# Longer rows for two weight loads, another way to turn the head outputs into columns, and a reordered middle, in a one-token decode block

## The chip, the cores and the metric

The kernel runs on one core of a Trainium2 chip. The metric is the device time of one execution in microseconds (us). Each kernel was executed several times. Every execution has its own span (first to last instruction, about 1.8 us shorter than the time) and its own mean granted clock of TensorE.

The executions of these kernels do not lie around one value: they fall into groups one to three microseconds apart. The label "fast" or "slow" that an execution carries is given by a rule (over 1.5% above the fastest execution of the same kernel is slow).

## The reference, cut to what matters

One token `x` of 576 values is normalised; its result feeds an attention over the last 4,096 positions of a cache (32 query heads on 16 key/value heads of 128) and a gated MLP. The results are added.

```python
xn = layernorm(x)                                   # 1 x 576
q  = xn @ wq                                        # 576 x 4096
p  = softmax(q . K[last 4096] / sqrt(128))          # 16 kv heads, 2 queries each
o  = p . V[last 4096]                               # 32 heads x 128
z  = gelu(xn @ w_in)                                # 576 x 4608, halves z1 and z2
h  = z1 * (w_sp * layernorm(z2) + b_sp)
out = x + o @ wo + h @ w_out                        # 4096 x 576, 2304 x 576
```

All data are bfloat16. Nearly all of the 51 MB that are read are read once: K and V are 33.6 MB, the four weight matrices 17.4 MB.

## The kernel before: the parts that matter

All large loads are issued from the SP queue, in one order that is the order of use: wq, w_in, then K and V in four groups ("quads") of four kv heads, then w_out and wo. K and V tiles of 32 KB a partition share three buffers, so a load can be issued only after the last reader of the tile that lay in its buffer.

```python
KV_BUFS = 3
...
nc.sync.dma_start(wq_t[:], wrows(A_wq, 0, 4))
nc.sync.dma_start(wq_h[:], whalf(A_wq))
for t in range(2):
    nc.sync.dma_start(win_t[t][:], wrows(B_w_in, 2 * t, 2 * t + 2))   # 18 KB a partition each
nc.sync.dma_start(win_h[:], whalf(B_w_in))
load_k(0); load_k(1); load_v(0)
...
quad(0, lambda: gz.extend(z_columns()), lambda: z_gate(*gz))
load_k(2)                       # into the buffer of K0
quad(1, lambda: transpose_p(0), nothing)
load_v(1)                       # into the buffer of K1: waits for the end of quad 1
pv_quad(0)
transpose_p(1)
load_k(3)                       # into the buffer of V0
quad(2, lambda: o_rows(0), nothing)
load_v(2)
...
```

`quad(g)` transposes the K of quad g on TensorE and multiplies it with q; `z_columns` are 18 small fp32 matmuls that turn z into columns, with the GELU behind them. They stand in the middle of quad 0.

The tail, behind the last V:

```python
den = ...                       # sum of the softmax denominators: waits for a DVE reduce
o_rows(2)
pv_quad(3)
...
for n, (g, r0, r1) in enumerate(WO_CHUNKS):          # four pieces of 8 rows
    for r in range(r0, r1):
        project(oT_all[:, r, g:g + 1], wo_sb[n][:, r - r0, :])   # one row step: two matmuls, 256 and 320 columns
    spin(2 if n > 0 else 0)                          # dummy matmuls
```

`spin(n)` issues n dummy matmuls of 512 columns, which write an unused accumulator. They are there to keep TensorE's clock up.

The softmax here doesn't subtract the row's maximum and nothing guards it: scores larger than these inputs give would overflow.

Of the kernel before, what the change touches and what calls it, by code (L numbers as in the profile page):

```python
# [8 lines left out]
FP32 = mybir.dt.float32  # L9
BF16 = mybir.dt.bfloat16  # L10
ALU = mybir.AluOpType
ACT = mybir.ActivationFunctionType
AXX = mybir.AxisListType.X
# [3 lines left out]
D = 576  # L17
HQ = 32
# [4 lines left out]
F = 4608  # L23
# [10 lines left out]
NZ = 36  # L34
NZ1 = 18
KV_BUFS = 3
WO_CHUNKS = ((0, 0, 8), (1, 0, 8), (2, 0, 8), (3, 0, 8))
WOUT_CHUNKS = ((0, 0, 9), (1, 0, 5), (1, 5, 8), (1, 8, 9))


# [1 line left out]
def kernel(  # L42
# [14 lines left out]
    nc = tc.nc  # L57
    P = nc.NUM_PARTITIONS
# [13 lines left out]

    xrow = const.tile([1, D], BF16, name="xrow")
    sb_row = const.tile([1, 2], BF16, name="sb_row")
    nc.gpsimd.dma_start(xrow[:], x_flat)
    nc.gpsimd.dma_start(sb_row[:, 0:1], B_w_sp.flatten_outer_dims()[0:1, 0:1])
    nc.gpsimd.dma_start(sb_row[:, 1:2], B_b_sp.flatten_outer_dims()[0:1, 0:1])

    def wrows(src, t0, t1):
        return src[0:512, :].rearrange("(p t) c -> p t c", t=4)[:, t0:t1, :]  # L80
# [4 lines left out]
    wq_t = wpool.tile([P, 4, 4096], BF16, name="wq")  # L85
    wq_sb = [wq_t[:, t, :] for t in range(4)]
    wq_h = wpool.tile([P, 2048], BF16, name="wqh")
    win_t = [wpool.tile([P, 2, F], BF16, name=f"win{t}") for t in range(2)]
    win_sb = [win_t[t // 2][:, t % 2, :] for t in range(4)]
    win_h = wpool.tile([P, FH], BF16, name="winh")  # L90
    kn_tiles: dict = {}
    v_tiles: dict = {}
# [20 lines left out]

    nc.sync.dma_start(wq_t[:], wrows(A_wq, 0, 4))
    nc.sync.dma_start(wq_h[:], whalf(A_wq))
    for t in range(2):
        nc.sync.dma_start(win_t[t][:], wrows(B_w_in, 2 * t, 2 * t + 2))  # L117
    nc.sync.dma_start(win_h[:], whalf(B_w_in))
    load_k(0)
    load_k(1)  # L120
# [47 lines left out]
    def mean_rstd(stat_t, n, nm):  # L168
# [26 lines left out]
    nc.vector.reduce_sum(ind4[:], ident[:].rearrange("p (k h) -> p h k", h=4), axis=AXX)  # L195
    nc.vector.tensor_scalar_mul(
        own[:].rearrange("p (h e) -> p h e", e=2), ind4[:].unsqueeze(2).to_broadcast([P, 4, 2]), BIG)
    hmask = const.tile([P, 8], FP32, name="hmask")
    nc.vector.reduce_sum(hmask[:], ident[:].rearrange("p (h d) -> p h d", d=16), axis=AXX)
    psum_all = const.tile([P, HQ], FP32, name="psum_all")  # L200
    id4f = const.tile([P, 4], FP32, name="id4f")
    nc.vector.tensor_copy(id4f[:], ident[:, 0:P:32])
# [49 lines left out]
    def z_columns():  # L252
        zv = zrow[:].rearrange("p (c t) -> p t c", t=9)
        for t in range(9):
            nc.tensor.matmul(  # L255
                fin[:, MZ + 4 * t:MZ + 4 * t + 4], lhsT=zv[:, t, :], rhs=id4f[:], start=True, stop=True,
            )
        zsb = const.tile([P, NZ], FP32, name="zsb")
        nc.vector.tensor_copy(
            zsb[:].rearrange("p (i t) -> p i t", i=4),  # L260
            fin[:, MZ:MZ + NZ].rearrange("p (t i) -> p i t", i=4),
        )
        u = const.tile([P, NZ], FP32, name="u_gelu")
        nc.vector.tensor_mul(u[:], zsb[:], zsb[:])
        nc.vector.tensor_scalar(out=u[:], in0=u[:], scalar1=0.044715, scalar2=1.0, op0=ALU.mult, op1=ALU.add)
        nc.vector.tensor_mul(u[:], u[:], zsb[:])
        th = const.tile([P, NZ], FP32, name="th_gelu")
        nc.scalar.activation(th[:], u[:], ACT.Exp, scale=-2.0 * GELU_C)
        nc.vector.tensor_scalar_add(th[:], th[:], 1.0)
        nc.vector.reciprocal(th[:], th[:])  # L270
        G = const.tile([P, NZ], FP32, name="G_gelu")
        nc.vector.tensor_mul(G[:], th[:], zsb[:])
        statz = const.tile([P, 2], FP32, name="statz")
        nc.vector.reduce_sum(statz[:, 0:1], G[:, NZ1:NZ], axis=AXX)
        junk2 = work.tile([P, NZ1], FP32, name="junk")
        nc.vector.tensor_tensor_reduce(
            out=junk2[:], in0=G[:, NZ1:NZ], in1=G[:, NZ1:NZ], scale=1.0, scalar=0.0,
            op0=ALU.mult, op1=ALU.add, accum_out=statz[:, 1:2],
        )
        return G, statz  # L280
# [3 lines left out]
    def z_gate(G, statz):  # L284
        mvz = mean_rstd(statz, FH, "z")
        z2n = const.tile([P, NZ1], FP32, name="z2n")
        nc.vector.tensor_scalar(out=z2n[:], in0=G[:, NZ1:NZ], scalar1=mvz[:, 0:1], scalar2=mvz[:, 3:4],
                                op0=ALU.subtract, op1=ALU.mult)
        gv = const.tile([P, NZ1], FP32, name="gv")
        nc.vector.tensor_scalar(out=gv[:], in0=z2n[:], scalar1=sb_col[:, 0:1], scalar2=sb_col[:, 1:2],  # L290
                                op0=ALU.mult, op1=ALU.add)
        nc.vector.tensor_mul(hv[:], G[:, 0:NZ1], gv[:])

    w2pool = tc.alloc_tile_pool(name="w2pool", bufs=1, reuse_waits="tile")
    wo_sb = [w2pool.tile([P, r1 - r0, D], BF16, name=f"wo{g}_{r0}") for g, r0, r1 in WO_CHUNKS]
    wout_sb = [w2pool.tile([P, t1 - t0, D], BF16, name=f"wout{i}_{t0}") for i, t0, t1 in WOUT_CHUNKS]

    ptq = const.tile([P, 4, 2, 4, 32], BF16, name="ptq")
# [38 lines left out]
    def transpose_p(g):  # L337
        p_sb = p_tiles.pop(g)
        ptps = ps_t.tile([P, 8, P], BF16, name=f"ptps{g}", tag="tps")
        for b in range(2):  # L340
            for s in range(4):
                nc.tensor.transpose(ptps[:, 4 * b + s, :], p_sb[:, b, 128 * s:128 * (s + 1)], ident[:])
        for c in range(4):
            for b in range(2):
                nc.vector.tensor_tensor(  # L345
                    ptq[:, c, b, :, :].rearrange("p i (s x) -> p i s x", x=8),
                    ptps[:, 4 * b:4 * b + 4, :].rearrange("p s (i r) -> p i s r", i=4)[:, :, :, 8 * c:8 * c + 8],
                    own[:].unsqueeze(1).unsqueeze(1).to_broadcast([P, 4, 4, 8]),
                    ALU.min,
                )  # L350
        nc.vector.tensor_reduce(  # L351
            out=psum_all[:, 8 * g:8 * g + 8],
            in_=ptq[:].rearrange("p c b i (s x) -> p x (c b i s)", x=8),
            op=ALU.add, axis=AXX,
        )
# [24 lines left out]
    def quad(g, first, then):  # L380
        transpose_k(4 * g)
        first()
        for u in range(4 * g + 1, 4 * g + 4):
            transpose_k(u)
            if u == 4 * g + 1:
                then()
            scores(u - 1)
        scores(4 * g + 3)

    def pv_quad(g):  # L390
        for u in range(4 * g, 4 * g + 4):
            pv(u)
# [2 lines left out]
        pass  # L395

    gz: list = []
    quad(0, lambda: gz.extend(z_columns()), lambda: z_gate(*gz))
    load_k(2)
    quad(1, lambda: transpose_p(0), nothing)  # L400
    load_v(1)
    pv_quad(0)
    transpose_p(1)
# [11 lines left out]
            B_w_out[ZC * i:ZC * (i + 1), :].rearrange("(p t) n -> p t n", t=9)[:, t0:t1, :])  # L415

    load_wout(0)
    for n, (g, r0, r1) in enumerate(WO_CHUNKS):
        nc.sync.dma_start(
            wo_sb[n][:], A_wo[1024 * g:1024 * (g + 1), :].rearrange("(p r) n -> p r n", r=8)[:, r0:r1, :])  # L420
    for n in range(1, len(WOUT_CHUNKS)):
        load_wout(n)

    quad(3, lambda: o_rows(1), nothing)
    pv_quad(2)
    transpose_p(3)
    den = ps_t.tile([P, 512], FP32, name="den", tag="tps")
    nc.tensor.matmul(den[0:HQ, 0:1], lhsT=psum_all[:], rhs=ones_f[:, 0:1], start=True, stop=True)
    rden = const.tile([HQ, 1], FP32, name="rden")
    nc.vector.reciprocal(rden[:], den[0:HQ, 0:1])  # L430
    o_rows(2)
    pv_quad(3)
    def project(lhsT, rhs, first=False, last=False):
        for g, (c0, c1) in enumerate(halves):
            nc.tensor.matmul(  # L435
# [15 lines left out]
            project(hv[:, k:k + 1], wout_sb[n][:, t - t0, :], last=(k == NZ1 - 1))  # L451

    project(one_row[:, 0:1], xrow[:], first=True)
    o_rows(3)
    project_b(0, range(0, 5))
    spin(2)

    onb = const.tile([HQ, DH], BF16, name="onb")
    nc.vector.tensor_scalar_mul(onb[:], oall, rden[:])
    orep = w2pool.tile([HQ, 8, 8, 16], BF16, name="orep")  # L460
    orep_src = onb[:].rearrange("p (d r) -> p r d", r=8).unsqueeze(2).to_broadcast([HQ, 8, 8, 16])
    nc.vector.tensor_copy(orep[:, 0:4, :, :], orep_src[:, 0:4, :, :])
    nc.scalar.copy(orep[:, 4:8, :, :], orep_src[:, 4:8, :, :])
    oh = ps_t.tile([P, 8, 32], FP32, name="oh", tag="tps")
    for r in range(8):
        nc.tensor.matmul(
            oh[:, r, :], lhsT=orep[:, r, :, :].rearrange("p h d -> p (h d)"), rhs=ident[0:HQ, 0:HQ],
            start=True, stop=True)
    project_b(0, range(5, 9))
    spin(2)  # L470
    om = w2pool.tile([P, 32, 8], FP32, name="om")
    nc.vector.tensor_mul(
        om[:], oh[:].rearrange("p r (g h) -> p (r g) h", h=8), hmask[:].unsqueeze(1).to_broadcast([P, 32, 8]))
    oT_all = const.tile([P, 8, 4], BF16, name="oT_all")
    with nc.allow_low_precision("one of the eight addends is not zero"):
        nc.vector.reduce_sum(oT_all[:].rearrange("p r g -> p (r g)"), om[:], axis=AXX)

    for n, (g, r0, r1) in enumerate(WO_CHUNKS):
        for r in range(r0, r1):
            project(oT_all[:, r, g:g + 1], wo_sb[n][:, r - r0, :])  # L480
        spin(2 if n > 0 else 0)
    for n in range(1, len(WOUT_CHUNKS)):
        project_b(n, range(WOUT_CHUNKS[n][1], WOUT_CHUNKS[n][2]))
        spin(1 if n == 1 else 0)
# [36 lines left out]
```

## Time and profile before

| | before |
|---|---|
| median of the first 6 executions | 129.09 us (127.38 to 130.18) |
| those 6, sorted | 127.38, 127.68, 128.46, 129.72, 130.09, 130.18 |
| profiled execution | 127.53 us, span 125.7, in the lower group |
| first bulk packet starts, last ends | 1.74 us, 122.47 us |

From the profile's page, before: the span, then in 40 slices the granted clock of TensorE and the busy share of the DMA engines (tenths), the DMA queue's packets, MB and share of 16 engines, and the chain of work that ended last.

```profile
span 125.7 us, 2492 instructions
PEclk9999999975559599999999999995589997699999
DMA  5998999899999899999999989899899999999970
q1 hardware_dynamic: 3314, 50.96, 95.3%
DMA 57%; PE 25%; DVE 8%; ACT 5%; SPq 2%; issue 1%; ACTq 0%
```

The DMA engines are busy all the time. 50.96 MB in the 120.7 us of the stream are 422 GB/s. With each packet's bytes spread evenly over its duration, more than half of the single microseconds have 430 to 434 GB/s and none has more. The Trainium skill, "DMA: Bandwidth & Descriptors", section "Where 436 GB/s comes from", gives 435 GB/s as the ceiling of the ports into the on-chip memory, and this trace agrees with it. (The same section says that for loads from HBM a limit near 358 GB/s binds instead; this trace of one core does not show that.)

From the timeline, before: start, length, engine, line, operation, and in brackets how long the engine was idle just before and what ended that. The first line is the issue of the second V load ("V1") on the SP queue. The others are TensorE's first use of the third K load ("K2"), the wait for the denominators, the first step on the last piece of wo, the last matmul, and the cast of the result.

```profile
62.17 0.54 SPq L102 DMA_DIRECT2D v_781<-in_A_v_cache_dram  x1
66.81 0.40 PE L310 MATMUL ktps_0_837<-ident,kn_550 128*128 128x128 bf16 x4 [0.82 <-DMA kn_550<-in_A_k_cache_dram]
105.61 0.24 PE L428 MATMUL den<-ones_f,psum_all 128*32 128x1 f32 x2 [3.30 <-DVE psum_all L351]
119.61 0.27 PE L435 MATMUL sps_118<-wo_0_297,oT_all 128*1 128x256 bf16 x1 [1.49 <-DMA wo_0_297<-in_A_wo_dram]
122.90 0.30 PE L435 MATMUL sps_119<-wout_8_301,hv 128*1 128x320 bf16 x1
123.23 0.42 ACT L488 CAST res<-sps_119 1x320 bf16<-1x320 f32 x1 [9.90 <-PE sps_119 L435]
```

The last matmul ends 0.7 us after the last bytes have landed (122.47 us).

### The profile page before, as it was taken

To read this page: it belongs to the slowest core of one execution; us is meant where nothing else is said; L and a number is where in the kernel's file an instruction comes from. 1 tells how busy PE (TensorE), PEld (TensorE's weight loads), DVE (VectorE), ACT (ScalarE), POOL (GpSimd) and SP (SyncE) were. 2 spreads that over 40 slices of the span, in tenths; PEclk is the share of its full clock that TensorE was granted. 3 is DMA by queue.
4 is the path that set the end of the run, shared out by engine and by line. 5 is a ranking of instruction groups with operands and counts; after the bars stand their busy time and mean duration, and the time that the engine had idled before them with its cause. 6 is when DMAs were issued, how large, how long until landed. Compare 5 with 4: busy or idle time off the path is not lost.

```text
span 125.7 us, 2492 instructions
## 1 busy us (share of the span) xinstructions
PE 82.4 (66%) x1091; PEld 61.0 (49%) x1091; DVE 45.1 (36%) x124; ACT 41.9 (33%) x50; POOL 3.5 (3%) x11
## 2 busy tenths in 40 slices
PE   0010268260599969997997999605999953968561
PEld 0000123120599948686747786305878523646340
DVE  3000622030120658399509844362245346022001
ACT  4000001010060338895863688200638920040001
POOL 6100010000000010000000000000000000000000
PEclk9999999975559599999999999995589997699999
DMA  5998999899999899999999989899899999999970
GB/s 167 396 438 364 459 434 446 380 451 433 433 454 490 365 480 412 417 461 391 469 396 433 469 365 495 386 448 469 360 454 404 427 421 417 427 434 416 421 280 0
DMA packets 3420, 51.11 MB, mean 407 GB/s; under 512 B 465, under 2 KB 594, under 8 KB 1106
## 3 DMA queue, kind: packets, MB, share of 16 engines
q1 hardware_dynamic: 3314, 50.96, 95.3%
q8 instruction: 8, 0.13, 0.4%
q0 software_dynamic: 96, 0.00, 0.0%
q14 instruction: 2, 0.02, 0.0%
HBM read 50.96 MB, written 0.00 MB: 405 GB/s over the span
## 4 chain that ended last, share of the span: by engine, by line
DMA 57%; PE 25%; DVE 8%; ACT 5%; SPq 2%; issue 1%; ACTq 0%
DMA kn_96<-in_A_k_cache_dram 24%; DMA wout_5_300<-in_B_w_out_dram 17%; DMA v_1106<-in_A_v_cache_dram 16%; PE fin L255 3%; DVE psum_all L351 3%; PE ops L363 3%; PE sps_119 L326 2%; DVE ptq L345 2%; PE sps_118 L326 1%; SPq L117 1%; PE ktps_0_303 L310 1%; ACT kT_3_1031 L314 1%; ACT kT_3_529 L314 1%; ACT kT_3_760 L314 1%; PE ktps_0_372 L310 1%
## 5 line engine op out<-in xcount | busy, mean ns | idle before, releaser
L310 PEld LDWEIGHTS <-kn_96 128*128 128x128 bf16 x128 | 10.5, 125 | 6.9 <-DMA kn_96<-in_A_k_cache_dram 6.1
L310 PEld LDWEIGHTS <-kn_835 128*128 128x128 bf16 x128 | 8.8, 112 | 7.0 <-DMA kn_835<-in_A_k_cache_dram 5.8
L310 PEld LDWEIGHTS <-kn_99 128*128 128x128 bf16 x128 | 7.2, 98 | 2.2 <-issue 2.1
L310 PEld LDWEIGHTS <-kn_550 128*128 128x128 bf16 x128 | 7.2, 98 | 2.1 <-issue 1.0
L351 DVE TENSOR_REDUCE psum_all<-ptq 128x8 f32<-128x1024 bf16 x4 | 7.9, 1966 | 0.1
L218 ACT CAST qrow<-sps_119 128x512 bf16<-128x512 f32 x1 | 0.6, 585 | 18.8 <-PE sps_119 L212 18.8
L363 PEld LDWEIGHTS <-ptq 128*32 128x32 bf16 x128 | 4.8, 103 | 2.7
L148 PE MATMUL fin<-one_row,xrow 1*128 1x1 bf16 x4 | 0.3, 172 | 8.2 <-DMA xrow<-in_A_x_dram 8.2
L326 PEld LDWEIGHTS <-q_bf 128*32 128x32 bf16 x128 | 3.0, 95 | 4.5 <-issue 2.8
L435 PEld LDWEIGHTS <-oT_all 128*1 128x1 bf16 x64 | 3.4, 83 | 3.1 <-issue 2.1
L310 PE MATMUL ktps_0_1117<-ident,kn_835 128*128 128x128 bf16 x8 | 1.0, 311 | 5.6 <-DMA kn_835<-in_A_k_cache_dram 5.6
L310 PE MATMUL ktps_0_303<-ident,kn_96 128*128 128x128 bf16 x8 | 1.0, 310 | 5.5 <-DMA kn_96<-in_A_k_cache_dram 5.5
L255 PEld LDWEIGHTS fin<-id4f,zrow 128*128 128x128 f32 x18 | 4.4, 336 | 0.0
L255 PE MATMUL fin<-id4f,zrow 128*128 128x4 f32 x18 | 4.4, 377 | 0.0
L148 PEld LDWEIGHTS <-xrow 1*128 1x128 bf16 x4 | 0.2, 113 | 8.2 <-DMA xrow<-in_A_x_dram 8.2
L488 ACT CAST res<-sps_119 1x320 bf16<-1x320 f32 x1 | 0.4, 416 | 9.9 <-PE sps_119 L435 9.9
L212 PE MATMUL sps_118<-wq,xz 128*32 128x512 bf16 x16 | 2.6, 628 | 1.6 <-DVE xz L181 1.6
L314 ACT COPY kT_1_1137<-ktps_1_1128 128x1024 bf16<-128x1024 bf16 x1 | 1.0, 1012 | 7.5 <-PE ktps_1_1128 L310 7.5
L487 DVE CAST res<-sps_118 1x256 bf16<-1x256 f32 x1 | 0.4, 412 | 8.6 <-PE sps_119 L435 8.6
L443 PE MATMUL spare<-wout_0_298,ident 128*32 128x512 bf16 x11 | 3.4, 385 | 0.0
L314 ACT COPY kT_1_323<-ktps_1_314 128x1024 bf16<-128x1024 bf16 x1 | 1.0, 1012 | 7.2 <-PE ktps_1_314 L310 7.2
L240 PEld LDWEIGHTS <-xz 128*32 128x32 bf16 x60 | 1.6, 96 | 3.7 <-issue 3.1
(339 smaller groups left out, 207.6 us busy)
## 6 DMA issues: line engine op xcount, KB each, us to landing
wq<-in_A_wq_dram SPq DMA_DIRECT2D x1, 4096.0 KB, 12.5
kn_96<-in_A_k_cache_dram SPq DMA_DIRECT2D x2, 2048.0 KB, 31.8
kn_99<-in_A_k_cache_dram SPq DMA_DIRECT2D x1, 4096.0 KB
v_101<-in_A_v_cache_dram SPq DMA_DIRECT2D x1, 4096.0 KB, 43.9
kn_550<-in_A_k_cache_dram SPq DMA_DIRECT2D x1, 4096.0 KB, 16.3
v_781<-in_A_v_cache_dram SPq DMA_DIRECT2D x1, 4096.0 KB, 14.2
kn_835<-in_A_k_cache_dram SPq DMA_DIRECT2D x1, 4096.0 KB, 20.6
v_1052<-in_A_v_cache_dram SPq DMA_DIRECT2D x1, 4096.0 KB, 19.1
```

The costliest lines, as they stand in the source:

```text
L117: nc.sync.dma_start(win_t[t][:], wrows(B_w_in, 2 * t, 2 * t + 2))
L212: nc.tensor.matmul(sps[b][32 * i:32 * i + 32, :], lhsT=lhsT, rhs=rhs, start=(t == 0), stop=(t == 4), tile_position=(0, 32 * i),)
L240: nc.tensor.matmul(zps[b][32 * i:32 * i + 32, 0:ZB], lhsT=lhsT, rhs=rhs, start=(t == 0), stop=(t == 4), tile_position=(0, 32 * i),)
L255: nc.tensor.matmul(fin[:, MZ + 4 * t:MZ + 4 * t + 4], lhsT=zv[:, t, :], rhs=id4f[:], start=True, stop=True,)
L310: nc.tensor.transpose(tps[:, s, :], kn[:, 32 * c + 8 * f + s, :], ident[:])
L314: nc.scalar.copy(kT[:], src)
L326: nc.tensor.matmul(sps[b][32 * i:32 * i + 32, :], lhsT=q_bf[:, g, c, :], rhs=parts[f // 2][:, 512 * (f % 2):512 * (f % 2) + 512], start=(c ...
L345: nc.vector.tensor_tensor(ptq[:, c, b, :, :].rearrange("p i (s x) -> p i s x", x=8), ptps[:, 4 * b:4 * b + 4, :].rearrange("p s (i r) -> p ...
L351: nc.vector.tensor_reduce(out=psum_all[:, 8 * g:8 * g + 8], in_=ptq[:].rearrange("p c b i (s x) -> p x (c b i s)", x=8), op=ALU.add, axis=AXX,
L363: nc.tensor.matmul(ops[32 * i:32 * i + 32, :], lhsT=ptq[:, c, b, i, :], rhs=v[:, t0:t0 + 4, :], start=(c == 0 and b == 0), stop=(c == 3 an ...
L435: nc.tensor.matmul(outp[g], lhsT=lhsT, rhs=rhs[:, c0:c1], start=first, stop=last, tile_position=(0, 32 * g),)
L443: nc.tensor.matmul(spare[64:96, :], lhsT=ident[:, 0:32], rhs=wout_sb[0][:, 0, 0:512], start=True, stop=True, tile_position=(0, 64))
```

## The change

The intent: fewer and longer rows for the DMA engines (w_in in one load of 36 KB rows, wo in two loads of 18 KB rows), a shorter chain from the head outputs to the projection (four small "placing" matmuls instead of two spread copies, eight matmuls, a multiply and a reduce), the z columns in a wait instead of inside quad 0, and the denominators behind the last PV instead of ahead of it.

```diff
-WO_CHUNKS = ((0, 0, 8), (1, 0, 8), (2, 0, 8), (3, 0, 8))
+WO_CHUNKS = ((0, 16), (16, 32))
...
-    nc.gpsimd.dma_start(xrow[:], x_flat)                  # and the two scalars
+    nc.scalar.dma_start(xrow[:], x_flat)
...
-    for t in range(2):
-        nc.sync.dma_start(win_t[t][:], wrows(B_w_in, 2 * t, 2 * t + 2))
+    nc.sync.dma_start(win_t[:], wrows(B_w_in, 0, 4))
...
-    hmask = const.tile([P, 8], FP32, name="hmask")
-    nc.vector.reduce_sum(hmask[:], ...)
+    place = const.tile([HQ, 4, P], BF16, name="place")
+    nc.gpsimd.memset(place[:], 0.0)
+    nc.gpsimd.affine_select(out=place[:], in_=place[:], ...)
...
-    quad(0, lambda: gz.extend(z_columns()), lambda: z_gate(*gz))
+    gz.extend(z_columns())
+    quad(0, nothing, nothing)
     load_k(2)
-    quad(1, lambda: transpose_p(0), nothing)
+    quad(1, lambda: transpose_p(0), lambda: z_gate(*gz))
...
-        wo_sb[n] <- A_wo[1024 * g:1024 * (g + 1), :].rearrange("(p r) n -> p r n", r=8)[:, r0:r1, :]
+        wo_sb[n] <- A_wo.rearrange("(p r) n -> p r n", r=32)[:, r0:r1, :]
...
+    o_rows(2)
+    pv_quad(3)
     den = ...
-    o_rows(2)
-    pv_quad(3)
...
-    orep copies, 8 matmuls oh[:, r, :], om = oh * hmask, oT_all = sum(om)
+    for d in range(4):
+        nc.tensor.matmul(oh[:], lhsT=place[:, d, :], rhs=onb[:, 32 * d:32 * d + 32], start=(d == 0), stop=(d == 3))
+    nc.vector.tensor_copy(oT_all[:], oh[:])
...
-            project(oT_all[:, r, g:g + 1], wo_sb[n][:, r - r0, :])
-        spin(2 if n > 0 else 0)
+            project(oT_all[:, r:r + 1], wo_sb[n][:, r - r0, :])
+            if r % 8 == 7:
+                spin(2 if r > 7 else 0)
```

(The two wo lines are shortened; the loads are as before from the SP queue. Where a row is left out, the diff has "...". Also left out: the nine row steps on the first w_out load, which fill waits of the tail, are split 2, 4 and 3 instead of 5 and 4, and the two `spin(2)` between them are now `spin(1)`, so the tail has two dummy matmuls fewer.)

More of the change, by code (lines that the diff above doesn't have):

```diff
@@ L74 @@
     sb_row = const.tile([1, 2], BF16, name="sb_row")
-    nc.gpsimd.dma_start(xrow[:], x_flat)
-    nc.gpsimd.dma_start(sb_row[:, 0:1], B_w_sp.flatten_outer_dims()[0:1, 0:1])
-    nc.gpsimd.dma_start(sb_row[:, 1:2], B_b_sp.flatten_outer_dims()[0:1, 0:1])
+    nc.scalar.dma_start(xrow[:], x_flat)
+    nc.scalar.dma_start(sb_row[:, 0:1], B_w_sp.flatten_outer_dims()[0:1, 0:1])
+    nc.scalar.dma_start(sb_row[:, 1:2], B_b_sp.flatten_outer_dims()[0:1, 0:1])
     def wrows(src, t0, t1):
@@ L87 @@
     wq_h = wpool.tile([P, 2048], BF16, name="wqh")
-    win_t = [wpool.tile([P, 2, F], BF16, name=f"win{t}") for t in range(2)]
-    win_sb = [win_t[t // 2][:, t % 2, :] for t in range(4)]
+    win_t = wpool.tile([P, 4, F], BF16, name="win")
+    win_sb = [win_t[:, t, :] for t in range(4)]
     win_h = wpool.tile([P, FH], BF16, name="winh")
@@ L197 @@
         own[:].rearrange("p (h e) -> p h e", e=2), ind4[:].unsqueeze(2).to_broadcast([P, 4, 2]), BIG)
-    hmask = const.tile([P, 8], FP32, name="hmask")
-    nc.vector.reduce_sum(hmask[:], ident[:].rearrange("p (h d) -> p h d", d=16), axis=AXX)
+    place = const.tile([HQ, 4, P], BF16, name="place")
+    nc.gpsimd.memset(place[:], 0.0)
+    nc.gpsimd.affine_select(
+        out=place[:], in_=place[:], compare_op=ALU.not_equal, fill=1.0, base=0,
+        pattern=[[1, 4], [-1, P]], channel_multiplier=4)
     psum_all = const.tile([P, HQ], FP32, name="psum_all")
@@ L294 @@
     w2pool = tc.alloc_tile_pool(name="w2pool", bufs=1, reuse_waits="tile")
-    wo_sb = [w2pool.tile([P, r1 - r0, D], BF16, name=f"wo{g}_{r0}") for g, r0, r1 in WO_CHUNKS]
+    wo_sb = [w2pool.tile([P, r1 - r0, D], BF16, name=f"wo{r0}") for r0, r1 in WO_CHUNKS]
     wout_sb = [w2pool.tile([P, t1 - t0, D], BF16, name=f"wout{i}_{t0}") for i, t0, t1 in WOUT_CHUNKS]
@@ L417 @@
     load_wout(0)
-    for n, (g, r0, r1) in enumerate(WO_CHUNKS):
-        nc.sync.dma_start(
-            wo_sb[n][:], A_wo[1024 * g:1024 * (g + 1), :].rearrange("(p r) n -> p r n", r=8)[:, r0:r1, :])
+    for n, (r0, r1) in enumerate(WO_CHUNKS):
+        nc.sync.dma_start(wo_sb[n][:], A_wo.rearrange("(p r) n -> p r n", r=32)[:, r0:r1, :])
     for n in range(1, len(WOUT_CHUNKS)):
@@ L453 @@
     project(one_row[:, 0:1], xrow[:], first=True)
+    project_b(0, range(0, 2))
     o_rows(3)
-    project_b(0, range(0, 5))
-    spin(2)
+    project_b(0, range(2, 6))
+    spin(1)
     onb = const.tile([HQ, DH], BF16, name="onb")
     nc.vector.tensor_scalar_mul(onb[:], oall, rden[:])
-    orep = w2pool.tile([HQ, 8, 8, 16], BF16, name="orep")
-    orep_src = onb[:].rearrange("p (d r) -> p r d", r=8).unsqueeze(2).to_broadcast([HQ, 8, 8, 16])
-    nc.vector.tensor_copy(orep[:, 0:4, :, :], orep_src[:, 0:4, :, :])
-    nc.scalar.copy(orep[:, 4:8, :, :], orep_src[:, 4:8, :, :])
-    oh = ps_t.tile([P, 8, 32], FP32, name="oh", tag="tps")
-    for r in range(8):
-        nc.tensor.matmul(
-            oh[:, r, :], lhsT=orep[:, r, :, :].rearrange("p h d -> p (h d)"), rhs=ident[0:HQ, 0:HQ],
-            start=True, stop=True)
-    project_b(0, range(5, 9))
-    spin(2)
-    om = w2pool.tile([P, 32, 8], FP32, name="om")
-    nc.vector.tensor_mul(
-        om[:], oh[:].rearrange("p r (g h) -> p (r g) h", h=8), hmask[:].unsqueeze(1).to_broadcast([P, 32, 8]))
-    oT_all = const.tile([P, 8, 4], BF16, name="oT_all")
-    with nc.allow_low_precision("one of the eight addends is not zero"):
-        nc.vector.reduce_sum(oT_all[:].rearrange("p r g -> p (r g)"), om[:], axis=AXX)
-    for n, (g, r0, r1) in enumerate(WO_CHUNKS):
+    oh = ps_t.tile([P, 32], FP32, name="oh", tag="tps")
+    for d in range(4):
+        nc.tensor.matmul(
+            oh[:], lhsT=place[:, d, :], rhs=onb[:, 32 * d:32 * d + 32], start=(d == 0), stop=(d == 3))
+    oT_all = const.tile([P, 32], BF16, name="oT_all")
+    nc.vector.tensor_copy(oT_all[:], oh[:])
+    project_b(0, range(6, 9))
+    spin(1)
+    for n, (r0, r1) in enumerate(WO_CHUNKS):
         for r in range(r0, r1):
-            project(oT_all[:, r, g:g + 1], wo_sb[n][:, r - r0, :])
-        spin(2 if n > 0 else 0)
+            project(oT_all[:, r:r + 1], wo_sb[n][:, r - r0, :])
+            if r % 8 == 7:
+                spin(2 if r > 7 else 0)
     for n in range(1, len(WOUT_CHUNKS)):
```

## The prediction

> # Prediction
>
> **What bounds the kernel now.** The DMA engines. The page shows 51.0 MB over the 125.7 us span, the sixteen engines 95.3% busy on one queue. In the trace's DMA records the first packet starts 1.7 us into the span, the last bulk packet ends at 122.4, and almost every microsecond between carries 423 to 434 GB/s. That agrees with the ceiling of 435 GB/s in the Trainium skill, "DMA: Bandwidth & Descriptors", section "Where 436 GB/s comes from". The chain of waits is 57% DMA. The tail is 3.3 us: last projections end at 123.2, cast to 123.65, store landed by 125.7.
>
> Every refill is issued before the queue runs dry: the third K load at 50.4 us (timeline) while the first V load lands at about 57; the others have 3 to 15 us to spare. TensorE time won in the middle starts no byte earlier.
>
> **The change, costed.**
> - Longer packets. DMA records: 51 ns (1,152 B), 347 (9,216 B), 686 (18,432 B), 1,213 (32,768 B), a line of 8 ns plus 0.0368 ns a byte. w_in goes from 256 packets to 128, wo from 512 to 256: 384 x 8 ns / 16 engines = 0.19 us less stream. Only this is on the critical path.
> - x and scalars leave the GpSimd queue (scalars landed at 13.07 us, q started at 16.87, wq was there at 13.2). q starts 3.5 us earlier, but z waits for all of w_in (25.2 us), on a cold TensorE.
> - The z columns (18 fp32 matmuls, 4.4 us) leave quad 0 for the 5.5 us wait before the first K. Transposes start 0 to 2 us later; quad 0 ends at 47 to 48 us rather than 51.9. Absorbed by the wait for the third K at 66.8.
> - Denominators after the last PV: TensorE now idles from 102.3 to 105.6, drops to half clock, ends PV at 109.9. It will end near 106.5.
> - o to columns: two spread copies (0.60, 1.09), 8 matmuls, multiply and reduce (0.42 each), 2.4 us in all, become 4 small matmuls and a copy, about 0.8. wo's first half lands only at about 114: absorbed.
> - Against it: the last wo piece is 16 rows instead of 8, landing at about 119.4. Then 16+5+3+1 = 25 steps at 0.137 us (timeline) remain: 3.4 us, ending near 123.0, beside 123.2 today. TensorE becomes as late as the last w_out bytes (122.5).
>
> **Critical path:** 0.2 us of DMA, less 0 to 0.2 us of backlog; span about 125.5 us. The runs of before lie near 127.5 and near 130, which I can't explain; a new set may fall on either side. I predict **128.5 us, 127.0 to 130.3**. Faster by over 2%: 0.03; within 2%: 0.92; slower: 0.05.
>
> **What would show it.** Right: stream 0.1 to 0.3 us shorter at the same rate; the tail's long PE wait is on the second wo half, then none or short ones; quad 0 over by 48 us but a longer third-K wait; last PV over by 107. Wrong: a stream shorter by over 0.5 us, or late refills.
>
> **What would make it wrong.** (1) Between the wo halves TensorE idles about 3 us. The Trainium skill, "TensorE: Matmul & The Clock Gate", Part 1, halves the clock after an idle window of about 3.4 us; this trace agrees (0.50 after 5.5 and 3.3 us idle). A cold tail doubles 25 steps: +3.4 us in some executions. (2) Rows of 36,864 bytes might be cut or move slower. (3) The slow runs of before may come from a tail that the change cures: the median falls to about 127.3.

## The result

| | before | changed |
|---|---|---|
| median, executions | 129.75 us, 20 | 129.60 us, 10 |
| lower group | 9 executions, 127.38 to 128.46 | 2 executions, 128.03 and 128.14 |
| upper group | 11 executions, 129.72 to 131.40 | 8 executions, 129.30 to 130.00 |
| ratio of the fast runs | | 1.012 (95%: 1.008 to 1.016) |
| profiled execution | 127.53, lower group | 128.21, lower group |
| last bulk packet ends | 122.47 us | 123.11 us |

The ratio is the mean time of the changed kernel's fast runs over that of the fast runs of before in the same rounds, so it is not quite the ratio of the medians. Here it needs care. The upper group of before is over 1.5% above its fastest execution and counts as slow. The upper group of the changed kernel is 1.0 to 1.5% above its own fastest, so nearly all of it counts as fast. The 1.012 compares the lower group of the one with mainly the upper group of the other. The medians differ by 0.1%. Group by group: the lower group went up by about half a microsecond (most of its executions were near 127.6, now 128.1), the mean of the upper group came down by 0.6 us (130.24 to 129.63), and the groups turn out to have different causes.

From the page of the changed kernel, the lines that answer to those of before:

```profile
span 126.4 us, 2476 instructions
PEclk9999996556855999999975799995599999778699
DMA  6998999799999999999999999999999999999960
q1 hardware_dynamic: 2882, 50.96, 95.1%
DMA 63%; PE 30%; SPq 2%; ACT 2%; issue 1%; DVE 0%; ACTq 0%
```

The same bytes with 432 records fewer, and yet the stream is not shorter. From its timeline, the issue of V1, the first use of K2, the first step on the second half of wo, the last matmul and the cast:

```profile
58.24 0.54 SPq L102 DMA_DIRECT2D v_780<-in_A_v_cache_dram  x1
66.97 0.82 PE L312 MATMUL ktps_0_836<-ident,kn_538 128*128 128x128 bf16 x6 [4.91 <-DMA kn_538<-in_A_k_cache_dram]
120.40 0.27 PE L437 MATMUL sps_116<-wo_296,oT_all 128*1 128x256 bf16 x1 [1.85 <-DMA wo_296<-in_A_wo_dram]
123.67 0.30 PE L437 MATMUL sps_117<-wout_8_300,hv 128*1 128x320 bf16 x1
124.01 0.42 ACT L483 CAST res<-sps_117 1x320 bf16<-1x320 f32 x1 [16.04 <-PE sps_117 L437]
```

V1 is issued 3.9 us sooner than before and TensorE waits 4.9 us for K2 instead of 0.8: what it gained in quad 0 it spends waiting, as predicted. But the last piece of wo is there 0.8 us later, and everything behind it is 0.8 us later too. The row steps behind it follow without a wait, so the chain that ends last now hangs on this piece (wo_296, 28% of the span in the page's list) and no longer on the last loads of w_out (wout_5, 17% before).

The reason for the later stream is in the DMA records of the trace, which give each packet's start, duration and size. The table has, for each kind of packet, the median duration in ns.

| packet (bytes), load | before | changed |
|---|---|---|
| 32,768, wq | 1,213 | 1,213 |
| 18,432 / 36,864, w_in | 686 | 1,364 |
| 16,384, K0 and last V | 611 | 614 |
| 32,768, all other K and V | 1,213 | 1,216 |
| 10,368, first w_out load | 389 | 396 |
| 9,216 / 18,432, wo | 347 | 689 |

A line of 8 ns plus 0.0368 ns a byte fits every number of before, and the changed kernel's w_in. It would give 686 for wo's 18,432 bytes. In the changed kernel each packet of K, V and wo takes 3 ns too long, and those of the first w_out load 7; the loads ahead of K0 and the last three of w_out (220, 135 and 51 ns) are unchanged. By the end of the last V the changed stream is 0.54 us behind (105.18 against 105.72 us), by its end 0.64.

### The profile page after: what moved, and what is told of

Its sections match the earlier page's. It is cut to its first block, busy times and chain, and to the rows that moved or that the text cites. A ratio compares the mean times of both kernels' runs of the same rounds, so it can differ in the third digit from the quotient of the medians.

```text
span 126.4 us, 2476 instructions
## 1 busy us (share of the span) xinstructions
PE 85.5 (68%) x1085; PEld 63.1 (50%) x1085; DVE 43.6 (35%) x121; ACT 41.0 (32%) x49; POOL 2.8 (2%) x10
## 4 chain that ended last, share of the span: by engine, by line
DMA 63%; PE 30%; SPq 2%; ACT 2%; issue 1%; DVE 0%; ACTq 0%
DMA wo_296<-in_A_wo_dram 28%; DMA win<-in_B_w_in_dram 19%; DMA kn_538<-in_A_k_cache_dram 16%; PE fin L257 4%; PE sps_117 L437 2%; PE zps_223 L242 1%; PE ops L365 1%; PE zps_225 L242 1%; PE zps_224 L242 1%; PE fin L377 1%; PE sps_116 L328 1%; PE sps_117 L328 1%; PE sps_116 L437 1%; PE ktps_0_836 L312 1%; ACT kT_3_1030 L316 1%; PE ktps_0_327 L312 1%
## 5 line engine op out<-in xcount | busy, mean ns | idle before, releaser
L312 PEld LDWEIGHTS <-kn_538 128*128 128x128 bf16 x128 | 8.7, 111 | 6.1 <-DMA kn_538<-in_A_k_cache_dram 5.1
L312 PEld LDWEIGHTS <-kn_834 128*128 128x128 bf16 x128 | 8.7, 110 | 5.3 <-DMA kn_834<-in_A_k_cache_dram 4.0
L312 PEld LDWEIGHTS <-kn_94 128*128 128x128 bf16 x128 | 9.9, 120 | 0.8 <-issue 0.8
L312 PEld LDWEIGHTS <-kn_97 128*128 128x128 bf16 x128 | 7.2, 98 | 2.0 <-issue 2.0
L437 PEld LDWEIGHTS <-oT_all 128*1 128x1 bf16 x64 | 4.2, 94 | 5.3 <-issue 4.3
L242 PEld LDWEIGHTS <-xz 128*32 128x32 bf16 x60 | 2.6, 143 | 8.5 <-issue 6.7
L242 PE MATMUL zps_223<-win,xz 128*32 128x384 bf16 x16 | 2.2, 519 | 6.7 <-DMA win<-in_B_w_in_dram 6.7
L365 PEld LDWEIGHTS <-ptq 128*32 128x32 bf16 x128 | 4.0, 96 | 4.5 <-issue 2.0
L312 PE MATMUL ktps_0_836<-ident,kn_538 128*128 128x128 bf16 x8 | 1.0, 311 | 4.9 <-DMA kn_538<-in_A_k_cache_dram 4.9
L249 ACT COPY zrow<-zps_224 128x384 f32<-128x384 f32 x1 | 0.5, 478 | 11.7 <-PE zps_224 L242 11.7
L248 DVE COPY zrow<-zps_223 128x384 f32<-128x384 f32 x1 | 0.6, 558 | 10.6 <-PE zps_223 L242 10.6
L437 PE MATMUL sps_116<-wo_295,oT_all 128*1 128x256 bf16 x16 | 2.8, 348 | 1.7 <-DMA wo_295<-in_A_wo_dram 1.7
L437 PE MATMUL sps_117<-wo_295,oT_all 128*1 128x320 bf16 x16 | 3.7, 407 | 0.0
```

Source lines behind the costliest of these rows:

```text
L242: nc.tensor.matmul(zps[b][32 * i:32 * i + 32, 0:ZB], lhsT=lhsT, rhs=rhs, start=(t == 0), stop=(t == 4), tile_position=(0, 32 * i),)
L248: nc.vector.tensor_copy(zrow[:, 0:ZB], zps[0][:, 0:ZB])
L249: nc.scalar.copy(zrow[:, ZB:2 * ZB], zps[1][:, 0:ZB])
L312: nc.tensor.transpose(tps[:, s, :], kn[:, 32 * c + 8 * f + s, :], ident[:])
L365: nc.tensor.matmul(ops[32 * i:32 * i + 32, :], lhsT=ptq[:, c, b, i, :], rhs=v[:, t0:t0 + 4, :], start=(c == 0 and b == 0), stop=(c == 3 an ...
L437: nc.tensor.matmul(outp[g], lhsT=lhsT, rhs=rhs[:, c0:c1], start=first, stop=last, tile_position=(0, 32 * g),)
```

## Experiments

All ran on one core, correct in every case. Runs of one call (1 to 4, 5 to 8, 9 to 12) share the executions of before. The three calls ran on three different chips, so times are compared within a call; the median durations of the large packets of one kernel were the same to the nanosecond on all of them. In each call the executions of before again fell into two groups: 6 of 11 were in the upper one in the first call (five by the rule, and one at 129.33 just below its limit), 4 of 13 in the second, 4 of 11 in the third.

At first two theories stood against each other. **A:** the cost is in the tail, where wo's second half brings 16 row steps at once and TensorE's clock may have dropped while it waited. **B:** the DMA stream itself is longer. A third, **C,** blamed the single w_in load.

### 1. The changed kernel again

No edit.

> The changed kernel unaltered, for the spread of its times and a second profile. Theory A (the tail): the second half of wo brings 16 row steps instead of 8 after the stream's last large piece, and an idle TensorE between the halves; the profile will show the last matmul 0.3 us or more after the last w_out bytes in a slow-mode execution, and the DMA stream ending within 0.3 us of the one of before (about 122.4 us). Theory B (the stream): the DMA stream itself ends later, by 0.5 to 2 us, and the matmuls end right behind it. Times expected again in two groups, near 128.1 and near 129.6 us; before near 127.5 and 130.

Measured: 127.99, 128.17, 128.31, 128.52, 129.43, 129.74 us, so two groups again, in other shares than in the result (4 and 2, after 2 and 8). The packets repeated to the nanosecond: 614, 1,216, 396, 689; the last one ended at 123.24 us. So the lower group goes with a longer stream (B), reproducibly. The upper group is not explained, because no profile fell into it here.

### 2. wo in four pieces, in the new layout

```diff
-WO_CHUNKS = ((0, 16), (16, 32))
+WO_CHUNKS = ((0, 8), (8, 16), (16, 24), (24, 32))
```

> The changed kernel with wo in four loads of 9 KB rows (8 rows each, same layout of 32 rows a partition), all else as changed. Theory A: the backlog after the last wo piece falls from 25 to 17 row steps, so the lower group of times moves from 128.1 to about 127.5 us and the upper group thins out. Theory B with the piece size as cause (longer rows slow the stream): same. Theory C (w_in or the early part is the cause): no change, 128.1 and 129.6.

Measured: 128.37, 128.38, 128.43, 128.45, 128.74 and 129.18 us. The lower group did not move to 127.5: it is not the row steps behind the last piece that raised it. The packets are again long (351 ns for 9,216 bytes, where before had 347), the last one ends at 123.15 us. So the size of the wo pieces is not what lengthens the stream.

### 3. The changed kernel with its tail kept warm

`warm(n)` is n dummy matmuls as in `spin`, but reading a V tile that is already there.

```diff
     project(one_row[:, 0:1], xrow[:], first=True)
+    warm(6)
...
-    spin(1)
+    warm(6)                          # ahead of the first half of wo
...
-                spin(2 if r > 7 else 0)
+                warm({7: 0, 15: 12, 23: 2, 31: 2}[r])
```

> The changed kernel with 24 more dummy matmuls of 512 columns (0.215 us each at full clock) in the three waits of the tail, 12 of them between the wo halves, so that TensorE never idles for long and keeps its clock. They read a V tile. Theory A with the clock as cause of the slow group: times gather near 127.5 to 128.1 us. Theory B: no change of the two groups, the granted clock in the tail is 1.0 all the same.

Measured: 128.03 to 128.25 us in all six executions; in the profiled one the granted clock in the tail was 1.00 throughout. The upper group did not appear. That makes the clock in the tail its likely cause. The lower value stays (the last packet ended at 123.11 us), as B says. Both theories are right, each for another group.

### 4. The kernel before with w_in in one load

```diff
-    for t in range(2):
-        nc.sync.dma_start(win_t[t][:], wrows(B_w_in, 2 * t, 2 * t + 2))
+    nc.sync.dma_start(win_t[:], wrows(B_w_in, 0, 4))
```

> The kernel before with only w_in turned into one load of 36 KB rows. Theory A: no change against before (ratio 0.995 to 1.005). Theory C (w_in in one load costs): the ratio of the fast runs goes to about 1.005 to 1.012.

Measured: ratio 1.006 (0.998 to 1.013), 128.33 to 129.56 us. The times fit C, but the trace does not: all later packets are as in before (611, 1,213, 389, 347 ns), the last one ends at 122.61 us. What makes the profiled execution 0.9 us longer is mainly the clock, which fell to half at 121.8 us, so that the last nine row steps ran until 124.1 us instead of 123.2. Why none of its six executions is near 127.5 stayed open. C as a cost of the stream falls.

What else could lengthen the packets from K0 on? The addresses of the built program (they stand in no trace) give a hint. The small tile `place` takes 1,024 bytes a partition and replaces one of 32 bytes. All large tiles therefore lie 992 bytes higher: K0 at 31,200 instead of 30,208. Before, all but two small w_out tiles start at multiples of 256; in the changed kernel every one starts 32 bytes off a multiple of 64. Call this **theory P** (place). Its rival **Q** blames the scalar queue, which now carries three small loads.

### 5. The kernel before with its tail kept warm

Twelve dummy matmuls ahead of the denominators, four and one more behind the last two pieces of wo.

```diff
     transpose_p(3)
+    warm(12)
     den = ...
...
-        spin(2 if n > 0 else 0)
+        warm((0, 2, 6, 3)[n])
```

> The kernel before with dummy matmuls added in the waits of its tail (12 before the denominators, 4 and 1 more behind the last two wo pieces), nothing else. If the slow group of before (about 129.7 to 131 us, more than half of its runs) is a TensorE at half clock in the tail, as the warm form of the changed kernel suggests, all runs fall to 127.3 to 127.7 us. If the slow group lies in the stream, it stays as it is.

Measured: 127.59, 127.65, 127.73 and 129.59, 129.79, 130.06, 130.17 us. The expectation failed: the tail ran at full clock and the slow group is still there. So the slow group of before is not the slow tail that the changed kernel has.

The profile fell into the slow group this time. It shows the execution that the profile of before had missed. The kernel is unaltered up to 104 us, so what happens earlier is before's own doing. From its timeline, the issue of V1:

```profile
63.59 0.54 SPq L102 DMA_DIRECT2D v<-in_A_v_cache_dram  x1
```

From its windows, four stretches (start and end in us, length, busy time and instructions of TensorE's matmuls and weight loads, of VectorE, ScalarE and GpSimd, granted clock, DMA share, GB/s):

```profile
42.00:46.00 4.00, 3.04 (x26) 1.92 (x24) 2.10 (x10) 2.01 (x3) 0.26 (x1) 0.50 0.93 401
46.00:50.00 4.00, 4.00 (x47) 3.47 (x44) 2.06 (x5) 1.54 (x2) 0.29 (x1) 0.62 0.95 406
62.00:66.00 4.00, 3.79 (x67) 2.52 (x67) 1.38 (x2) 3.23 (x5) 0.00 (x0) 1.00 1.04 385
66.00:70.00 4.00, 4.00 (x63) 3.27 (x54) 2.51 (x9) 2.19 (x3) 0.00 (x0) 1.00 0.98 373
```

The same stretches in the fast execution of before:

```profile
42.00:46.00 4.00, 3.02 (x31) 2.33 (x29) 2.44 (x12) 2.16 (x3) 0.00 (x0) 0.75 0.97 418
46.00:50.00 4.00, 4.00 (x72) 3.47 (x69) 2.67 (x8) 2.33 (x3) 0.55 (x1) 1.00 0.94 406
62.00:66.00 4.00, 3.78 (x59) 1.82 (x56) 0.42 (x1) 2.87 (x5) 0.00 (x0) 1.00 1.01 434
66.00:70.00 4.00, 3.11 (x43) 2.84 (x44) 3.94 (x11) 1.98 (x3) 0.00 (x0) 1.00 1.08 463
```

In the slow execution TensorE was at half clock until 49 us, in the fast one until 44. Quads 0 and 1 ended later, and V1 was issued at 63.59 instead of 62.17 us. The moving rate then falls from 434 and 463 to 385 and 373 GB/s. (The view counts a packet whole where it starts, so a stretch can read too high; spread evenly, it is 430 and 428 against 373 and 331.) The DMA records show it packet by packet: from 64.50 us on the engines finish their parts of K2 and have nothing more to do, the first packet of V1 starts at 64.93 (1.34 us after the start of the issue), and just before that only 4 of the 16 engines have a packet in flight.

Worse, the packets with which the dry engines start again take 1.75 to 2.3 us instead of 1.21, and one behind them 2.6, much as the first packets of the kernel do (1.3 to 2.3 us). In the fast execution only about one packet in each later load of K or V is that slow (1.7 us). The last packet ends at 124.54 us, 2.1 us later than in the fast execution. This is **theory L**: the slow group of before is a late refill.

Even in the fast execution the first engine is done with K2 at about 64.5 us, nearly 2 us before the last one (66.4), so the spare time was never the four and a half microseconds that the timeline seemed to show (V1 is issued at 62.17 us and K2 is in use at 66.81).

### 6. The kernel before with 992 unused bytes

```diff
+    pad = const.tile([P, 248], FP32, name="pad")
+    nc.vector.memset(pad[:], 0.0)
     psum_all = const.tile([P, HQ], FP32, name="psum_all")
```

> The kernel before with an unused tile of 992 bytes a partition ahead of the large buffers, which moves their addresses to where the changed kernel has them (remainder 32 by 64, 224 by 256). Theory P (place of the destination): packets of K and V take 1,216 and 614 ns instead of 1,213 and 611, those of the first w_out load about 397 instead of 389, and the stream ends about 0.5 us later than in before (last w_out load at about 122.9 to 123.1 us). Theory Q (the scalar queue): 1,213, 611, 389 as before, end at 122.4 to 122.6.

Measured: ratio 1.008 (1.006 to 1.011). Packets of 614, 1,216, 396 and 351 ns; the last ended at 123.41 us, 0.9 us later than before's. Theory P holds so far as it says that the shift lengthens the packets, and Q is not needed: nothing was moved to the scalar queue here. Two limits: the pad moves every tile that is allocated behind it, the engines' working tiles too, so the runs do not show that it is the start of the DMA's destination that counts. And the start alone can't be enough: in the changed kernel the first half of wo lies at the very address that wq had (149,984), and wq's packets were not slower.

### 7. The changed kernel with 32 unused bytes

```diff
+    pad = const.tile([P, 8], FP32, name="pad")
+    nc.vector.memset(pad[:], 0.0)
```

> The changed kernel with an unused tile of 32 bytes a partition, which makes the addresses of all large buffers multiples of 512 again. Theory P: packets 1,213, 611, 389, 686 ns, stream about 0.5 to 0.6 us shorter (last w_out load ends at about 122.4 to 122.6 us), the lower group of times at about 127.4 to 127.6, the upper group (cold tail) still there near 129. Theory Q: packets stay at 1,216, 614, 397, 689 and times at 128.1 and 129.6.

Measured: 127.28, 127.39, 127.47, 127.51 and 128.73, 128.74 us. Packets of 611, 1,213, 389 and 686 ns; the last ended at 122.50 us. The pad took 0.6 us from the stream and about 0.6 from the lower group. It also shows what the longer rows are worth when nothing is in their way: from the end of the wq loads to the end of the large w_in loads the trace has 10.89 us here and 10.93 before, and for wo 10.93 and 11.01. That is 0.12 us where 0.19 had been estimated, close to the resolution of such a reading.

### 8. The changed kernel with the small loads back on GpSimd

```diff
-    nc.scalar.dma_start(xrow[:], x_flat)          # and the two scalars
+    nc.gpsimd.dma_start(xrow[:], x_flat)
```

> The changed kernel with its three small loads back on the GpSimd queue. Theory Q: packets of the large loads back at 1,213, 611, 389 and 686 ns and the stream 0.5 us shorter. Theory P: packets stay at 1,216, 614, 397, 689 and the times at 128.1 and 129.6.

Measured: 128.56, 128.67, 129.88, 130.12 us; packets 614, 1,216, 396, 689. Theory Q falls. The profile fell into the upper group of the changed kernel, which no other had shown so far. Its windows in the tail (the third number from the end is the granted clock):

```profile
119.00:121.00 2.00, 0.46 (x5) 0.35 (x6) 0.00 (x0) 0.00 (x0) 0.00 (x0) 0.71 0.91 370
121.00:123.00 2.00, 2.00 (x22) 1.56 (x20) 0.00 (x0) 0.00 (x0) 0.00 (x0) 0.50 0.56 213
```

From its timeline, the first step on the second half of wo and the cast of the result:

```profile
120.54 1.50 PE L437 MATMUL sps<-wo,oT_all 128*1 128x256 bf16 x11 [3.19 <-DMA wo<-in_A_wo_dram]
125.44 0.42 ACT L483 CAST res<-sps 1x320 bf16<-1x320 f32 x1 [17.35 <-PE sps L437]
```

TensorE idled 3.19 us between the halves of wo, its clock fell to half from 119.8 to 123.2 us, and the 25 row steps and the cast that follow needed 4.9 us to reach the point that took 3.6 us in the lower group (120.40 to 124.01 us). That is 1.3 us, most of the 1.4 between the two groups of this run. It fits the clock: half clock for the 2.7 us from 120.54 to 123.2 costs half of them. Run 12, the other profile of an upper group, has its half clock from 120.0 to 123.5 us; in the lower group's profiles with the same tail (the result's, runs 1 and 7) it ended by 119.2.

In the lower group the same gap is crossed by luck. There the half clock came while the first half of wo was being used, which made the wait after it shorter, and the clock was up again in time. The windows of the profile after:

```profile
115.00:117.00 2.00, 2.00 (x25) 1.70 (x23) 0.00 (x0) 0.00 (x0) 0.00 (x0) 0.68 1.02 433
117.00:119.00 2.00, 1.55 (x12) 0.57 (x8) 0.00 (x0) 0.00 (x0) 0.00 (x0) 0.50 0.96 405
119.00:121.00 2.00, 0.60 (x12) 0.55 (x14) 0.00 (x0) 0.00 (x0) 0.00 (x0) 0.97 0.93 381
```

The Trainium skill, "TensorE: Matmul & The Clock Gate", Part 1, says why luck enters: the clock is set from windows of about 3.4 us that run freely, not counted from the kernel's start. The traces agree: the stretches of half clock here begin at different times and are 3.4 us long, or two to four times that (13.65 us in run 6).

### 9. The kernel before with only the z columns moved

```diff
-    quad(0, lambda: gz.extend(z_columns()), lambda: z_gate(*gz))
+    gz.extend(z_columns())
+    quad(0, nothing, nothing)
     load_k(2)
-    quad(1, lambda: transpose_p(0), nothing)
+    quad(1, lambda: transpose_p(0), lambda: z_gate(*gz))
```

> The kernel before with only the z columns moved ahead of quad 0 and the z gate into quad 1. Theory L (late refill: the slow group of before is the second V load, issued too late when TensorE was at half clock for long in quad 0): the second V load is issued at 58 to 60 us instead of 62 to 63.6, the slow group of 129.6 to 131 us is gone, all runs between 127.4 and 128.4 us. If the slow group has another cause, about half of the runs are still over 129.5 us.

Measured: 127.50, 127.51, 127.56, 127.56, 127.72 us, while before had 4 of 11 executions between 129.55 and 130.03 in the same rounds. From the timeline, the issue of V1:

```profile
59.35 0.54 SPq L102 DMA_DIRECT2D v<-in_A_v_cache_dram  x1
```

The slow group did not appear, with an edit that touches nothing but the work ahead of that issue. Five executions alone could be chance (with 4 slow ones in 11, five fast ones in a row come one time in ten); but the twelve executions of runs 3 and 10, which also have this move and a warm tail, had none of this group either. The ratio of the fast runs is 0.999, because it leaves the slow ones out: by the fast runs alone this edit is worth nothing, and by the mean of all executions of these rounds (127.57 against 128.50 us) it is worth 0.7%.

### 10. Both cures in the changed kernel

The 32 bytes of run 7 and the `warm` lines of run 3.

> The changed kernel with both cures: 32 unused bytes, so that the large buffers start at multiples of 512, and the dummy matmuls in the tail's waits. All runs in one group at 127.3 to 127.6 us, ratio to the fast runs of before 0.995 to 1.0, median 1 to 1.5% below the median of before in the same rounds when half of those are slow.

Measured: 127.19 to 127.52 us in six executions, median 127.36, one group; ratio 0.998 (0.996 to 0.999); median 0.35% below that of before in these rounds, where 4 of 11 executions of before were slow, and 1.8% below the 129.75 us of the result's 20, which were not of the same rounds. From the timeline, the first step on the second half of wo and the cast:

```profile
119.52 0.84 PE L439 MATMUL sps<-wo,oT_all 128*1 128x256 bf16 x11 [1.01 <-DMA wo<-in_A_wo_dram]
123.13 0.42 ACT L492 CAST res<-sps 1x320 bf16<-1x320 f32 x1 [15.86 <-PE sps L439]
```

And from its windows, one stretch of the tail, at full clock:

```profile
121.00:123.00 2.00, 2.00 (x32) 1.20 (x27) 0.00 (x0) 0.00 (x0) 0.00 (x0) 1.00 0.30 114
```

This is the best of all kernels here. From the wo piece to the cast it needs 3.6 us, and 25 row steps at 0.137 us are 3.4: the backlog that the prediction had counted.

### 11. The best kernel with V1 held back

28 dummy matmuls in quad 1, to hold back the issue of V1.

```diff
-    quad(1, lambda: transpose_p(0), lambda: z_gate(*gz))
+    quad(1, lambda: transpose_p(0), lambda: (z_gate(*gz), late()))    # late(): 28 dummy matmuls
```

> The same as the run with both cures, plus 28 dummy matmuls of 512 columns (6 us at full clock) in quad 1, which do nothing but hold back the second V load, to 63 to 64 us. Theory L: the DMA engines run dry near 65 us, the first packets after that take about 2 us, the stream ends 1.5 to 2.5 us later and all runs are at 129 to 130 us. If 3 us between issue and the end of the load before is enough, times stay at 127.3 to 127.6.

Measured: 128.27, 128.27, 128.32, 128.61, 129.15, 129.58 us. From the timeline, the issue of V1:

```profile
63.38 0.54 SPq L102 DMA_DIRECT2D v<-in_A_v_cache_dram  x1
```

From the windows, the stretch in which the engines run dry, at 320 GB/s:

```profile
64.00:66.00 2.00, 1.79 (x34) 0.84 (x31) 0.00 (x0) 1.55 (x3) 0.00 (x0) 1.00 0.89 320
```

With V1 issued at 63.38 us, its first packet starts at 64.71 (1.33 us later), the engines in use fall to 7 of 16 just before that and are 9 around 65 us, five first packets take 1.6 to 2.1 us, and the last packet ends at 123.12 us instead of 122.36. The mechanism is as L says, in a kernel that had one group only. The size was overstated: 0.9 us over run 10's median in three executions, 1.3 to 2.2 in the other three. Part of the larger ones may come from the tail, which was not warm throughout here (half clock from 115.9 to 119.3 us in the profiled one). The time lost depends steeply on when the issue comes: in the profiled executions 62.17 us cost nothing, 63.38 about 0.8 and 63.59 about 2 us.

### 12. The changed kernel with 96 unused bytes

```diff
+    pad = const.tile([P, 24], FP32, name="pad")
```

> The changed kernel with 96 unused bytes a partition: the large buffers start at multiples of 64 but not of 128 or 256. If a start off a 64-byte boundary is what costs, the packets are at 1,213, 611, 389 and 686 ns; if a multiple of 256 or 512 is needed, at 1,216, 614, about 396 and 689 as in the changed kernel.

Measured, one look: 129.61 us (upper group, half clock in the tail again). Neither expectation came in full. The packets are in between: 613, 1,215 and 688 ns, the first w_out load back at 389, but the second w_out load, which had 220 ns in before and in the changed kernel, now 228. A multiple of 64 is not enough, and the loads suffer differently. The exact rule stays open.

## Why the prediction was right or wrong

**Right.** The DMA engines bound the kernel, and the time that TensorE won in the middle was absorbed by a longer wait for K2 (0.8 us before, 4.9 after). The longer rows save 8 ns a packet, 0.12 us of 0.19 estimated (run 7). q started 2.9 us earlier (13.97 against 16.87 us; 3.5 predicted), quad 0's last matmul ended at 48.0 us (47 to 48 predicted), and the last PV at 107.3 (106.5 predicted). 25 row steps stand behind the last wo piece: 3.6 us from its first to the cast, 3.4 counted.

**Wrong, step 1: "Only this is on the critical path", 0.2 us less stream.** The sum lacked a term. The new constant tile moved every large buffer by 992 bytes, to starts that are no multiples of 64, and the stream became 0.6 us longer instead of 0.2 shorter. Run 6 puts that into before by 992 unused bytes, run 7 takes it out of the changed kernel by 32. This is the half microsecond by which the lower group rose.

**Wrong, step 2: "Every refill is issued before the queue runs dry ... the others have 3 to 15 us to spare. TensorE time won in the middle starts no byte earlier."** This was read from one execution of the fast group, as the distance from an issue to the landing of the load ahead of it. The engines finish a load nearly 2 us apart, and an issue needs about 1.3 us until its first packet moves. With the issue at 62.17 us and the first engine free at about 64.5, the real slack was about 1.0 us. In run 5's profile a longer stretch of half clock in quad 0 used it up (issue at 63.59); going by their times, it did so in 25 of all 55 executions of before. The z move brought V1's issue forward, by 2.8 us in run 9 and by 3.9 in the changed kernel, and cured that (run 9). So TensorE's time in the middle was worth about 2 us, in the executions that the profile had not shown. The prediction had said that it could not explain the two groups of before; its guess at a tail that the change cures named the wrong place.

**Right in kind, wrong in size, step 3: "A cold tail doubles 25 steps: +3.4 us in some executions."** It came, at 1.3 us (run 8), because the half clock lasted one window of 3.4 us and part of that lay in the wait; and it came in 8 of the 10 executions of the result and in 2 of 6 in runs 1 and 7, not as a rare risk.

Put together: minus 2 us in the slow half of before's executions, plus 0.6 in all for the addresses, plus 1.3 in most for the tail. The median came out where it had been, and that it lies near the prediction is luck: none of these three terms was in its sum, and its 128.5 us lay between two groups that it could not explain. The kernel changed a bad group that comes from the middle for a milder one that comes from the end.

Left open: why packets ahead of K0 (wq, w_in) do not suffer from their shifted addresses, whether it is the loads' own starts or those of the other shifted tiles that count, the exact rule of run 12, the share of each group, which differs from one set of executions to the next, why run 4 had no execution near 127.5 us, and why none of the ten executions of runs 4 and 6, which also have the z columns in quad 0, was near 130. That the slow group of unaltered before is the late refill was not seen in a trace of that very kernel; it rests on run 5 (the same program up to 104 us), on runs 9, 3 and 10, and on run 11.

## What to carry to other kernels

When executions fall into groups, get a profile of each group before costing a change: slack that is read from a fast execution is not slack. Count the spare time of a refill up to the first engine that runs dry, and take off the way from issue to first packet; a queue that ran dry pays again with slow first packets. And after any edit that adds or removes a small constant tile, look at where the large buffers now start; here the kernels whose K, V and wo tiles start at multiples of 512 bytes had the short packets in every trace.

## What the Trainium skill lacked or had wrong

- "DMA: Bandwidth & Descriptors", section "How a descriptor splits into AXI transactions", tells what a start that is no multiple of 256 bytes costs in terms of bytes read; it has no figure for shifted tiles in on-chip memory. Here a shift to 32 bytes off a multiple of 64 cost 3 ns on packets of 1,213 and 611 ns, 7 on 389, and 4 on 347 ns, and nothing on the loads at the start of the kernel and the last three of w_out: 0.6 to 0.9 us of a 121 us stream.
- The same page, in "Latency and other measured facts", gives about 600 ns to the first byte on this path. Here it was 1.34 and 1.33 us from the start of an issue to the first packet of a queue that had run dry (63.59 to 64.93 us in run 5, 63.38 to 64.71 in run 11), of which the issue itself is 0.54. No page says that the first packets after a dry spell are slow: 1.75 to 2.3 us instead of 1.21 in run 5.
- The same page, section "Rules for kernel authors", asks for few, large transfers, without a figure for longer rows in loads that are over 1 MiB already. Going from 18 KB to 36 KB rows (w_in) and from 9 KB to 18 KB (wo) saved 8 ns for each pair of packets made into one, 0.12 us in all (run 7).
- "TensorE: Matmul & The Clock Gate", Part 1, has the idle window right. It does not say that narrow matmuls may count as idling, which this case suggests and does not prove: in the kernel before, TensorE was busy without a break from 36.36 to 40.74 us with 18 fp32 matmuls of 4 columns, and its clock was at half from 40.6 to 44.0 us.
